# Attention and a mixture of experts on one core: the PSUM banks of sums and of turned sums in one pool of six

## The chip, the cores and the metric

The kernel runs on one core of a Trainium2 chip. The metric is the device time of one execution in microseconds (us); the median of three runs before the change is 2277.7 us (2277.5 to 2278.34). A measured change of less than about 0.2% can't be told from none.

## The reference

```python
def _attn_ref(u, v, z):                     # u, v: (8, 2496, 256), z: (8, 2496, 64)
    scores = (1.0 / S) * np.matmul(z, z.transpose(0, 2, 1))
    attn = np.maximum(scores, 0.0) ** 2
    return u * np.matmul(attn, v)

def _moe_ref(x, modality_id, w_gate, modality_bias, w1, w2):   # x: (19968, 256), 8 experts, F = 1024
    logits = x @ w_gate + modality_bias[modality_id]
    e_idx = np.argmax(logits, axis=1)
    probs = softmax(logits); gate_w = probs[np.arange(N), e_idx]
    for e in range(E):
        mask = e_idx == e
        h = np.maximum(x[mask] @ w1[e], 0.0)
        out[mask] = gate_w[mask, None] * (h @ w2[e])
```

The rows that the attention gives are the tokens of the experts.

## The kernel before

**The attention** runs over 8 batches of 2496 rows. A batch is cut into 5 chunks of queries, four of 512 columns and a last of 448, and every chunk goes through 10 steps over the keys, two key tiles of 128 a step (`i` from 0 to 9). A step has

- six score matmuls (`scores`, L280) into the two banks of the pool `ps_s`, issued three steps ahead of their use;
- on ScalarE the ReLU out of these banks (L288) and the square (L294);
- the split of the squares into a high and a low part, `ah` (L310, on ScalarE or VectorE) and `al` (L319, VectorE);
- 24 products (`weigh`, L335) with the high and low parts of `v`, summed over the 10 steps. They have 64 rows of contraction each, so two run at a time, one on either half of the array. There are four sums for a chunk, each in a bank of 512 float32: the two halves `r` of the contraction by the two halves `dh` of the 256 output rows.

At the first step of a chunk (`i == 0`) the products stand in the order of `dh`: twelve into the two sums of `dh = 0`, then twelve into those of `dh = 1`. That is the **change of chunk**. Around it stand, in this order on each engine:

- ScalarE, at the end of the old chunk: `evacuate_low` (L379) copies the two sums with `r = 1` to SBUF, `h = 0` first;
- VectorE, in the first step of the new chunk: `evacuate_high` (L383) adds the two sums with `r = 0` to these copies, `h = 1` first and `h = 0` last;
- TensorE, after the 24 products of that step: `make_rows` (L413) turns the sum by 16 transposes into two more banks, which VectorE reads in the next step (`take_rows`, L423).

Then come logits (L435), routing for each batch (`route_count` on TensorE, L512, into two banks, read by `route_slots`, L518 and L520) and the scatter of the rows to DRAM.

**The experts** follow: tiles of 512 tokens, with `up` (L1006) and `down` (L1019, L1020), in pools of their own, `ps_h` and `ps_o`, which take over the eight banks. Four tiles of one expert run before the general ones; the turned sums of the attention's last chunk (`make_last_rows`, L395) are made after the second `up` of the first of them.

**Banks.** The core has eight banks. In the attention two belong to `ps_s`, four to `ps_a` (the sums, tag `acc`) and two to `ps_t` (tag `po`: turned sums, route counts, the first warming matmuls, and a second set of scores at three places near the start). A pool hands out the bank that was given back first. The first instruction that writes a new tile waits until the last reader of the bank's tile before it is done; TensorE runs its instructions in program order, so all that is behind waits too. The order of instructions on all engines is written by the program (a planner in the code sets it when the program is built).

Of the kernel before, what the change touches and what calls it, by code (L numbers as in the profile page):

```python
# [9 lines left out]
F32 = mybir.dt.float32  # L10
# [5 lines left out]
P = 128  # L16
T = 512
PSUM = bass.MemoryType.PSUM
# [8 lines left out]
def tile_attention_moe(ctx: ExitStack, tc: tile.TileContext, u, v, zt, mid, wg, mb, w1, w2, out):  # L27
# [15 lines left out]
    E, _, F = w1.shape  # L43
    N = B * S
    KD, KF = D // P, F // P
# [34 lines left out]
    ph1, feed = ExitStack(), ExitStack()  # L80
# [3 lines left out]
    bulk = ph1.enter_context(tc.tile_pool(name="bulk", bufs=1))  # L84
    raw = feed.enter_context(tc.tile_pool(name="raw", bufs=1, side="right"))
    ps_s = ph1.enter_context(tc.tile_pool(name="ps_s", bufs=1, space=PSUM))
    ps_a = ph1.enter_context(tc.tile_pool(name="ps_a", bufs=4, space=PSUM))
    ps_t = ph1.enter_context(tc.tile_pool(name="ps_t", bufs=2, space=PSUM))
    bank = {"pool": ps_t, "tag": "po"}

    def bank_tile(shape, name):
        return bank["pool"].tile(shape, F32, tag=bank["tag"], name=name)
# [171 lines left out]
    acc = {}  # L264

    def scores(g, more=False):

        b, c, i = steps[g]
        w = width[c]
        if more:  # L270
            s = [bank_tile([P, T], "s") for _ in halves]
        else:
            both = ps_s.tile([P, 2, T], F32, tag="s", name="s")
            s = [both[:, t, :] for t in range(2)]
        mv = Z[b, c]
        for n, (kl, ql) in enumerate(((0, 1), (1, 0), (0, 0)) if g else ((0, 0), (0, 1), (1, 0))):
            for t in range(2):
                k = 2 * i + t
                lhs = Z[b, k // J][halves[t], kl, (k % J) * P:(k % J + 1) * P]
                nc.tensor.matmul(out=s[t][:, :w], lhsT=lhs, rhs=mv[halves[t], ql, :w], start=n == 0, stop=n == 2)  # L280
        r = bulk.tile([P, 2, T], F32, tag="a", bufs=3, name="r")
        if more or not g:
            for t in range(2):
                nc.scalar.activation(out=r[:, t, :w], in_=s[t][:, :w], func=AF.Relu, scale=INV)  # L284
                if not g:
                    nc.scalar.square(out=r[:, t, :], in_=r[:, t, :])
        else:
            nc.scalar.activation(out=r[:, :, :w], in_=both[:, :, :w], func=AF.Relu, scale=INV)  # L288
        st_s[g] = r
# [37 lines left out]
    def weigh(g, inside=()):  # L327
        b, c, i = steps[g]
        w = width[c]
        ah, al = st_h.pop(g)  # L330
        if i == 0:
            acc[b, c] = list(zip(*([ps_a.tile([P, T], F32, tag="acc", name="acc") for _ in range(2)] for _ in range(KD))))

        def product(r, dh, k, x, y, stop=False):
            nc.tensor.matmul(  # L335
                out=acc[b, c][r][dh][:, :w],
                lhsT=V[b, k // J][y][halves[r], k % J, dh * P:(dh + 1) * P],
                rhs=x[halves[r], k % 2, :w],
                start=k == 0 and x is ah and not y,
                stop=stop,  # L340
            )


        last = i == NI - 1
        terms = [(dh, x, y) for dh in range(KD) for x, y in ((ah, 0), (ah, 1), (al, 0))]
        if i or not g:
            terms.sort(key=lambda t: (t[1] is al, t[2]))
        tiles = (2 * i, 2 * i + 1)[:1 if last else 2]
        for ks in (tiles,) if g else ((k,) for k in tiles):
            for m, (dh, x, y) in enumerate(terms):  # L350
                if m == len(terms) - KD and 2 * i in ks:
                    for n in inside:
                        scores(n, True)
                for k in ks:
                    for r in range(2):
                        product(r, dh, k, x, y)
        if last:

            k = NCOL - 1
            product(1, 0, k, al, 0, True)  # L360
            product(0, 1, k, ah, 0, True)
            product(1, 1, k, al, 0)
            product(0, 0, k, ah, 0)
            product(1, 1, k, ah, 1, True)
            product(0, 0, k, ah, 1, True)
# [517 lines left out]
    with tc.manual_schedule(engines={ET.PE, ET.Activation, ET.DVE, ET.Pool}):  # L883
# [44 lines left out]
        for g in range(G):  # L928
            waiting += [(end, g, p) for end, p in due.pop(g, ())]
            b, c, i = steps[g]  # L930
# [28 lines left out]
            for n in new_s:  # L959
                clock["A"] += 1.05 * scale  # L960
                square(n)
            weigh(g, inside)
            for n in inside:
                after += 0.69
# [244 lines left out]
```

## Time and profile before

| | |
|---|---|
| median of three runs | 2277.7 us |
| the profiled execution | 2277.82 us |
| its span, first to last instruction | 2276.0 us |
| end of the attention's products | about 1375 us |
| TensorE matmuls busy | 2247.5 us, 99% |
| weight loads (PEld) busy | 2029.5 us, 89% |
| VectorE busy | 1807.1 us, 79% |
| ScalarE busy | 1574.1 us, 69% |
| GpSimd busy | 360.6 us, 16% |
| mean granted clock of TensorE | 0.997 |

PE are TensorE's matmuls, PEld its weight loads, which run ahead of the matmuls that use them; DVE is VectorE, ACT ScalarE, POOL GpSimd. In a row `acc<-ah,vh` the tile ahead of the arrow is written, those behind it are read. Times in a timeline are counted from the start of the span; what stands in brackets is the idle time of the engine just ahead of the row and what ended it. A matmul's length counts from its start to its modelled end, so that two that overlap are both busy.

### The profile page before, as it was taken

To read this page: it belongs to the slowest core of one execution; us is meant where nothing else is said; L and a number is where in the kernel's file an instruction comes from. 1 tells how busy PE (TensorE), PEld (TensorE's weight loads), DVE (VectorE), ACT (ScalarE), POOL (GpSimd) and SP (SyncE) were. 2 spreads that over 40 slices of the span, in tenths; PEclk is the share of its full clock that TensorE was granted. 3 is DMA by queue.
4 is the path that set the end of the run, shared out by engine and by line. 5 is a ranking of instruction groups with operands and counts; after the bars stand their busy time and mean duration, and the time that the engine had idled before them with its cause. 6 is when DMAs were issued, how large, how long until landed. Compare 5 with 4: busy or idle time off the path is not lost.

```text
span 2276.0 us, 44472 instructions
## 1 busy us (share of the span) xinstructions
PE 2247.5 (99%) x16874; PEld 2029.5 (89%) x16874; DVE 1807.1 (79%) x4552; ACT 1574.1 (69%) x1917; POOL 360.6 (16%) x349
## 2 busy tenths in 40 slices
PE   9999999999999999999999999999999999999996
PEld 7999999999999999999989998888888888888885
DVE  7889989989989989989989889766666666666663
ACT  7888888888888888888888873455455455555452
POOL 0000210210210210210110321411212121212111
PEclk9999999999999999999999999999999999999998
DMA  6222222222112112112111122644545454545440
GB/s 186 105 69 92 89 87 95 92 70 74 37 53 73 38 53 72 38 54 72 38 49 35 53 87 51 190 133 146 140 138 154 125 166 117 162 121 158 128 144 23
DMA packets 199602, 216.64 MB, mean 95 GB/s; under 512 B 118448, under 2 KB 166064, under 8 KB 194512
## 3 DMA queue, kind: packets, MB, share of 16 engines
q1 hardware_dynamic: 184288, 172.49, 26.2%
q0 software_dynamic: 15088, 41.21, 4.9%
q8 instruction: 134, 2.20, 0.4%
q14 instruction: 92, 0.75, 0.1%
HBM read 168.23 MB, written 62.19 MB: 101 GB/s over the span
## 4 chain that ended last, share of the span: by engine, by line
PE 61%; issue 25%; DMA 9%; POOL 3%; ACT 1%; DVE 1%; POOLq 0%; ACTq 0%; DVEq 0%
PE acc L335 46%; PE s L280 12%; DMA out_dram<-y,ids 9%; POOL out_dram L1038 3%; PE ph L1006 1%; PE po L413 1%; PE po L1019 1%; ACT r L288 0%; ACT r L294 0%; DVE spare L435 0%; PE po L1020 0%; POOLq L1038 0%; PE warm L887 0%; ACT x L379 0%; ACT r L284 0%
## 5 line engine op out<-in xcount | busy, mean ns | idle before, releaser
L288 ACT ACTIVATE r<-s 128x1024 f32<-128x1024 f32 (+1 forms) x395 | 397.9, 1007 | 217.1 <-PE s L280 216.8
L335 PE MATMUL acc<-ah,vh 64*128 64x512 f32 (+1 forms) x3120 | 530.1, 387 | 8.4 <-ACT x L379 7.1
L319 DVE TENSOR_TENSOR al<-r,ah 128x1024 fp32r<-128x1024 f32 (+1 forms) x359 | 430.3, 1199 | 111.5 <-ACT ah L310 96.9
L335 PE MATMUL acc<-ah,vl 64*128 64x512 f32 (+1 forms) x3120 | 511.8, 382 | 0.0
L335 PE MATMUL acc<-al,vh 64*128 64x512 f32 (+1 forms) x3120 | 506.7, 382 | 0.0
L435 DVE SCALAR_TENSOR_TENSOR spare<-x,wgb 128x256 f32<-128x256 f32 x1280 | 461.9, 419 | 1.0
L1010 ACT ACTIVATE hh<-ph 128x512 fp32r<-128x512 f32 x312 | 186.6, 598 | 386.7 <-PE ph L1006 346.2
L1019 PE MATMUL po<-w,hh 128*128 128x512 f32 x1256 | 450.0, 394 | 0.0
L335 PEld LDWEIGHTS acc<-ah,vh 64*128 64x128 f32 x3120 | 399.7, 184 | 48.0 <-ACT x L379 32.3
L1006 PE MATMUL ph<-xh,w 128*128 128x512 f32 x1248 | 429.9, 395 | 0.0
L294 ACT ACTIVATE r<-r 128x1024 f32<-128x1024 f32 (+1 forms) x399 | 415.8, 1042 | 3.5
L335 PEld LDWEIGHTS acc<-ah,vl 64*128 64x128 f32 x3120 | 403.6, 184 | 14.0
L335 PEld LDWEIGHTS acc<-al,vh 64*128 64x128 f32 x3120 | 403.0, 184 | 14.2
L280 PE MATMUL s<-zm 64*128 64x512 f32 (+1 forms) x2400 | 405.7, 385 | 0.8 <-ACT r L288 0.3
L1011 DVE SCALAR_TENSOR_TENSOR hl<-ph,hh 128x512 fp32r<-128x512 f32 x312 | 215.3, 690 | 218.1 <-ACT hh L1010 189.6
L548 POOL DMA_INDIRECT xs<-x,sloti x160 | 200.8, 1255 | 1052.5 <-DVE x L546 1006.9
L1020 PE MATMUL po<-w,hl 128*128 128x256 f32 x1256 | 351.5, 280 | 0.2 <-DVE hl L1011 0.2
L280 PEld LDWEIGHTS s<-zm 64*128 64x128 f32 x2400 | 310.8, 185 | 8.5 <-ACT r L288 0.8
L310 ACT CAST ah<-r 128x1024 fp32r<-128x1024 f32 (+1 forms) x283 | 288.1, 1018 | 0.0
L1019 PEld LDWEIGHTS po<-w,hh 128*128 128x128 f32 x1256 | 235.7, 188 | 55.4
L1006 PEld LDWEIGHTS ph<-xh,w 128*128 128x128 f32 x1248 | 234.2, 188 | 55.9 <-issue 0.3
L1038 POOL DMA_INDIRECT out_dram<-y,ids x157 | 152.8, 973 | 692.3 <-DVE y L1036 657.8
(155 smaller groups left out, 1982.5 us busy)
## 6 DMA issues: line engine op xcount, KB each, us to landing
w<-w1s SPq DMA_DIRECT2D x37, 1024.0 KB
w<-w2s SPq DMA_DIRECT2D x37, 1024.0 KB
xg<-xs SPq DMA_DIRECT2D x156, 128.0 KB
vr<-in_v_dram SPq DMA_DIRECT2D x32, 512.0 KB
ut<-in_u_dram SPq DMA_DIRECT2D x32, 512.0 KB
zr<-in_zt_dram SPq DMA_DIRECT2D x40, 256.0 KB
w1s<-in_moe_w_dram SPq DMA_DIRECT2D x16, 512.0 KB
w2s<-in_moe_w_dram SPq DMA_DIRECT2D x8, 1024.0 KB
```

The source lines that it names most:

```text
L280: nc.tensor.matmul(out=s[t][:, :w], lhsT=lhs, rhs=mv[halves[t], ql, :w], start=n == 0, stop=n == 2)
L288: nc.scalar.activation(out=r[:, :, :w], in_=both[:, :, :w], func=AF.Relu, scale=INV)
L294: nc.scalar.square(out=a[:, :, :w], in_=a[:, :, :w])
L310: copy(out=ah[:, :, :w], in_=st_a[g][:, :, :w])
L319: nc.vector.tensor_tensor(out=al[:, :, :w], in0=a[:, :, :w], in1=ah[:, :, :w].bitcast(F32), op=ALU.subtract)
L335: nc.tensor.matmul(out=acc[b, c][r][dh][:, :w], lhsT=V[b, k // J][y][halves[r], k % J, dh * P:(dh + 1) * P], rhs=x[halves[r], k % 2, :w], ...
L435: nc.vector.scalar_tensor_tensor(out=spare[:, k % 2, :], in0=x[:, j, 0:D], scalar=1.0, in1=wgb[:, e, :], op0=ALU.mult, op1=ALU.mult, accum ...
L1006: nc.tensor.matmul(out=ph, lhsT=lhs, rhs=rhs[:, k, :], start=n == 0, stop=n == 3 * KD - 1)
L1011: nc.vector.scalar_tensor_tensor(out=hl, in0=ph, scalar=0.0, in1=hh.bitcast(F32), op0=ALU.max, op1=ALU.subtract)
L1019: nc.tensor.matmul(out=po[j], lhsT=hh[:, s], rhs=both, start=f == 0, stop=False, skip_group_check=True)
L1020: nc.tensor.matmul(out=po[j][:, 0:D], lhsT=hl[:, s], rhs=w[:, 0, :], start=False, stop=f == KF - 1, skip_group_check=True)
L1038: nc.gpsimd.indirect_dma_start(out=out, out_offset=bass.IndirectOffsetOnAxis(ap=ids[:, j:j + 1], axis=0), in_=y, in_offset=None, bounds_ch ...
```

## The change

```diff
-    ps_a = ph1.enter_context(tc.tile_pool(name="ps_a", bufs=4, space=PSUM))
-    ps_t = ph1.enter_context(tc.tile_pool(name="ps_t", bufs=2, space=PSUM))
-    bank = {"pool": ps_t, "tag": "po"}
+    ps_a = ph1.enter_context(tc.tile_pool(name="ps_a", bufs=6, space=PSUM))
+    bank = {"pool": ps_a, "tag": "acc"}
...
         if i == 0:
-            acc[b, c] = list(zip(*([ps_a.tile([P, T], F32, tag="acc", name="acc") for _ in range(2)] for _ in range(KD))))
+            acc[b, c] = list(zip(*([bank_tile([P, T], "acc") for _ in range(2)] for _ in range(KD))))
```

The pools `ps_a` and `ps_t` become one of six banks, from which the sums, the turned sums, the route counts and the early scores all take the bank that was given back first. The program has one line less, so that L335 is L334 after the change, and so on. Every engine has the same instructions in the same order as before; what differs is the bank of a tile and with it what TensorE waits for. In the rows that follow, the engine that is waited for stands in brackets, and `x2` means two instructions alike.

TensorE at the change from the third to the fourth chunk of the first batch, before: six scores, 24 products, and the transposes into `po`.

```order
L280 MATMUL s<-zm 128x512 [waits Activation_49]
L280 MATMUL s<-zm 128x512 x5
L335 MATMUL acc<-ah,vh 128x512 [waits Activation_49] x2
L335 MATMUL acc<-ah,vh 128x512 x2
L335 MATMUL acc<-ah,vl 128x512 x4
L335 MATMUL acc<-al,vh 128x512 [waits DVE_49]
L335 MATMUL acc<-al,vh 128x512 x3
L335 MATMUL acc<-ah,vh 128x512 [waits DVE_49] x2
L335 MATMUL acc<-ah,vh 128x512 x2
L335 MATMUL acc<-ah,vl 128x512 x4
L335 MATMUL acc<-al,vh 128x512 x4
L413 MATMUL po<-ident,x 128x64 x16
```

The same place after the change:

```order
L279 MATMUL s<-zm 128x512 [waits Activation_49]
L279 MATMUL s<-zm 128x512 x5
L334 MATMUL acc<-ah,vh 128x512 x4
L334 MATMUL acc<-ah,vl 128x512 x4
L334 MATMUL acc<-al,vh 128x512 [waits DVE_49]
L334 MATMUL acc<-al,vh 128x512 x3
L334 MATMUL acc<-ah,vh 128x512 [waits Activation_49] x2
L334 MATMUL acc<-ah,vh 128x512 x2
L334 MATMUL acc<-ah,vl 128x512 x4
L334 MATMUL acc<-al,vh 128x512 x4
L412 MATMUL po<-ident,x 128x64 [waits DVE_49]
L412 MATMUL po<-ident,x 128x64 x15
```

The two waits for ScalarE's copies have moved from the first two products to the thirteenth and fourteenth, and the wait for VectorE's adds from these to the first transpose. It is so at all 39 changes of chunk; at six of them, each the first after a batch's route count, the first two products wait as well:

```order
L279 MATMUL s<-zm 128x512 x5
L334 MATMUL acc<-ah,vh 128x512 [waits DVE_49] x2
L334 MATMUL acc<-ah,vh 128x512 x2
L334 MATMUL acc<-ah,vl 128x512 x4
L334 MATMUL acc<-al,vh 128x512 [waits DVE_49]
```

What they wait for there is VectorE's reading of the counts (L518 and L520 of before). The last place is the end of the attention on TensorE: the last products, the first two `up` products of the first expert tile (six matmuls each) and the transposes of the last chunk; before the change

```order
L335 MATMUL acc<-ah,vl 128x448 x2
L1006 MATMUL ph<-xh,w_0_18698 128x512 [waits PE_49,Activation_49]
L1006 MATMUL ph<-xl,w_0_18698 128x512 [waits DVE_49]
L1006 MATMUL ph<-xh,w_0_18698 128x512 [waits DMAHW3_49]
L1006 MATMUL ph<-xh,w_0_18698 128x512 [waits Activation_49]
L1006 MATMUL ph<-xl,w_0_18698 128x512
L1006 MATMUL ph<-xh,w_0_18698 128x512 [waits DVE_49]
L1006 MATMUL ph<-xh,w_0_18698 128x512 [waits Activation_49]
L1006 MATMUL ph<-xl,w_0_18698 128x512
L1006 MATMUL ph<-xh,w_0_18698 128x512 x2
L1006 MATMUL ph<-xl,w_0_18698 128x512
L1006 MATMUL ph<-xh,w_0_18698 128x512
```

and after it:

```order
L334 MATMUL acc<-ah,vl 128x448 x2
L1005 MATMUL ph<-xh,w_0_18695 128x512 [waits PE_49,Activation_49]
L1005 MATMUL ph<-xl,w_0_18695 128x512 [waits DVE_49]
L1005 MATMUL ph<-xh,w_0_18695 128x512 [waits DMAHW3_49]
L1005 MATMUL ph<-xh,w_0_18695 128x512 [waits Activation_49]
L1005 MATMUL ph<-xl,w_0_18695 128x512
L1005 MATMUL ph<-xh,w_0_18695 128x512 [waits DVE_49] x2
L1005 MATMUL ph<-xl,w_0_18695 128x512
L1005 MATMUL ph<-xh,w_0_18695 128x512 x2
L1005 MATMUL ph<-xl,w_0_18695 128x512
L1005 MATMUL ph<-xh,w_0_18695 128x512
L394 MATMUL po<-ident,x 128x128 [waits Activation_49]
```

The seventh of these matmuls, the first of the second `up`, waited for ScalarE and now waits for VectorE: its bank held the sum with `r = 0`, `dh = 0` of the last chunk, which the last add (L383, `h = 0`) reads.

## The prediction

> **What bounds the kernel now.** First the page: span, busy shares and the 40 slices; then the waits, longest first; then the timeline at ordinary steps and at the change of chunk.
>
> ```profile
> span 2276.0 us, 44472 instructions
> ...
> PE 2247.5 (99%) x16874; PEld 2029.5 (89%) x16874; DVE 1807.1 (79%) x4552; ACT 1574.1 (69%) x1917; POOL 360.6 (16%) x349
> ...
> PEclk9999999999999999999999999999999999999998
> ```
>
> Then the windows view of the attention from its first change of chunk on (length, busy us of PE, PEld, DVE, ACT and POOL, granted clock, DMA share, GB/s):
>
> ```profile
> 42.00:1375.00 1333.00, 1325.75 (x12119) 1256.23 (x12117) 1181.27 (x3592) 1106.96 (x1222) 190.70 (x163) 1.00 0.21 67
> ```
>
> TensorE is busy 99% of the span, and in the attention 1325.75 of 1333 us with the full clock. That looks like nothing to gain. But a matmul that starts late while its predecessor drains still counts as busy, so busy time hides lost issue time. The waits show it (who <- for whom: total us, times, longest):
>
> ```profile
> ACT r L288 <- PE s L280: 216.8, 295, 2.5
> ...
> DVE al L319 <- ACT ah L310: 96.9, 120, 3.2
> ...
> PEld acc L335 <- ACT x L379: 32.3, 78, 1.4
> ...
> PE acc L335 <- ACT x L379: 7.1, 8, 0.9
> ...
> PEld acc L335 <- DVE x L383: 3.5, 16, 0.3
> ...
> PEld s L280 <- ACT r L288: 0.8, 1, 0.8
> ```
>
> ScalarE waits for TensorE (216.8 us), so TensorE sets the pace of the attention. TensorE itself waits at one place: the weight loads of the products (L335) wait 78 times, twice at each of the 39 changes of chunk, for ScalarE's copies of the previous chunk's sums (L379), and 16 times for VectorE's adds (L383). Together 32.3 + 3.5 = **35.8 us**. Whether those are lost is read from start to start. Two ordinary steps begin like this in the timeline, a step being six score matmuls and 24 products (start, length):
>
> ```profile
> 188.47 1.03 PE L280 MATMUL s<-zm 64*128 64x512 f32 x6
> ...
> 191.87 1.03 PE L280 MATMUL s<-zm 64*128 64x512 f32 x6
> ```
>
> So 30 matmuls of 512 columns take 3.40 us, 15 pairs of 0.227. Now a change of chunk:
>
> ```profile
> 284.72 1.03 PE L280 MATMUL s<-zm 64*128 64x512 f32 x6
> ...
> 285.10 1.05 ACT L379 COPY x<-acc 128x512 f32<-128x512 f32 x2
> ...
> 285.72 0.18 PEld L335 LDWEIGHTS acc<-ah,vh 64*128 64x128 f32 x1 [0.39 <-ACT x L379]
> ...
> 286.18 1.29 DVE L383 TENSOR_TENSOR x<-acc,x 128x512 f32<-128x512 f32 x2 [0.56 <-ACT x L379]
> 286.20 0.29 PEld L335 LDWEIGHTS acc<-ah,vh 64*128 64x128 f32 x3 [0.30 <-ACT x L379]
> ...
> 288.84 0.69 PE L413 MATMUL po<-ident,x 64*128 64x64 f32 x13
> ```
>
> From the scores to the transposes that follow the 24 products: 288.84 - 284.72 = 4.12 us instead of 3.40. The loss of 0.72 is the two waits, 0.39 + 0.30, and a little. Where ScalarE comes late, at the change of batch, more is lost:
>
> ```profile
> 178.91 1.22 DVE L250 TENSOR_TENSOR vl<-vr,vh 128x1024 fp32r<-128x1024 f32 x1
> ...
> 179.24 0.51 PE L335 MATMUL acc<-ah,vl 64*128 64x448 f32 x2
> 179.44 1.00 PE L280 MATMUL s<-zm 64*128 64x512 f32 x6
> ...
> 179.82 1.06 ACT L294 ACTIVATE r<-r 128x1024 f32<-128x1024 f32 x1
> ...
> 180.78 0.95 ACT L379 COPY x<-acc 128x448 f32<-128x448 f32 x2
> 181.35 0.18 PEld L335 LDWEIGHTS acc<-ah,vh 64*128 64x128 f32 x1 [1.34 <-ACT x L379]
> ...
> 181.77 1.16 DVE L383 TENSOR_TENSOR x<-acc,x 128x448 f32<-128x448 f32 x2 [0.50 <-ACT x L379]
> 181.79 0.29 PEld L335 LDWEIGHTS acc<-ah,vh 64*128 64x128 f32 x3 [0.25 <-ACT x L379]
> ...
> 184.47 0.69 PE L413 MATMUL po<-ident,x 64*128 64x64 f32 x13
> ...
> 186.11 1.03 ACT L288 ACTIVATE r<-s 128x1024 f32<-128x1024 f32 x1 [1.03 <-PE s L280]
> ```
>
> Here 184.47 - 179.44 = 5.03, a loss of 1.63 against waits of 1.34 + 0.25. So the idle of PEld at these waits is lost time nearly one to one, and the ceiling of the change is 35.8 us.
>
> **The change part by part.** No instruction is added, removed or moved; only the bank of each sum and what is waited for before its first matmul. At a change of chunk the first two new sums (rows dh=0) now take the two banks that held turned sums, the next two (dh=1) take the ones that ScalarE's copies free, and the turned sums take those that VectorE's adds free.
>
> *First two sums.* No wait is left: the turned sums are read (L423) in the step after they are written, most of a chunk ago. After a chunk with a route count the wait is for L518/L520, which read the counts:
>
> ```profile
> L520 DVE TENSOR_TENSOR base<-pc,base x17: 155/165/167, 243.9 to 1417.0; 128x8 f32<-128x8 f32 x17
> ...
> 250.93 0.18 PEld L335 LDWEIGHTS acc<-ah,vh 64*128 64x128 f32 x1 [0.39 <-ACT x L379]
> ```
>
> The first read of counts starts at 243.9, and the next chunk's first load stands at 250.93, or 0.7 earlier without its wait: about 6 us of cover. At a change of batch the second four products need a low part of `v`, written (L250) by 178.91 + 1.22 = 180.13 at the latest; without waits they come at 179.44 + 5 x 0.227 = 180.57. Cost nothing.
>
> *Last two sums.* They now wait for the copies, 12 products later. In the first example they are due at 284.72 + 9 pairs x 0.227 = 286.76, and the second copy released its bank by 286.20: 0.56 us of cover, so nothing is paid. At the change of batch they are due at 179.44 + 2.04 = 181.48, and the releases are at 181.35 and 181.79: the second one stays, some 0.3 us, less the 0.03 to 0.18 by which the second of a pair starts later anyway; I take 0.25. The seven changes of batch are of this kind, the first shown above and the last here, and one more change like them, at 1243.21:
>
> ```profile
> 1207.81 0.18 PEld L335 LDWEIGHTS acc<-ah,vh 64*128 64x128 f32 x1 [1.34 <-ACT x L379]
> ...
> 1243.21 0.18 PEld L335 LDWEIGHTS acc<-ah,vh 64*128 64x128 f32 x1 [1.19 <-ACT x L379]
> ```
>
> 8 x 0.25 = 2.0 us stay.
>
> *Turned sums.* The transposes now wait for VectorE's adds themselves, where before the products had waited. They read what the adds write, so no bank can be ready later than the data. In the first example the adds end at 286.18 + 1.29 = 287.47 and the transposes come to 284.72 + 3.40 = 288.12: cover 0.65. At the change of batch 182.93 against 183.09: cover 0.16, enough but thin. Behind this wait stand the next scores, so what is late here is paid in full; it would be what is late next.
>
> *What is late after that.* The next scores need the two banks of scores, read by L288; TensorE waited once for that in the whole run, 0.8 us. ScalarE's 216.8 us of waiting for scores shrink by what TensorE gains. VectorE is busy 1181.27 of 1333 us; with 33 us less it is at 91%, and no row of the waits has a product waiting for `al`, which is made three steps ahead.
>
> *End of the attention.* By the new banks the second up product of the first expert tile starts in the bank that the last add frees (it was one that a copy frees):
>
> ```profile
> 1375.65 0.50 PE L1006 MATMUL ph<-xh,w 128*128 128x512 f32 x1
> ...
> 1377.49 1.14 DVE L383 TENSOR_TENSOR x<-acc,x 128x448 f32<-128x448 f32 x2
> ...
> 1378.32 0.40 PE L1006 MATMUL ph<-xh,w 128*128 128x512 f32 x1
> 1378.69 0.86 PEld L395 LDWEIGHTS po<-ident,x 128*128 128x128 f32 x8 [0.41 <-DVE x L383]
> ```
>
> The first and the last of the twelve matmuls of two up products start 2.67 us apart, so one product of six takes about 1.4 us. The second ran while the adds did; now it must start after 1377.49 + 1.14 = 1378.63, and its 1.4 us stand ahead of the transposes of L395, which began at 1378.69. Lost once: 1.4 us, up to 2.0 if VectorE, with little slack there, does not follow the gain of the last chunk. I take 1.7.
>
> The sum: 35.8 - 2.0 - 1.7 = 32.1 us, all in the part before 1380 us. The expert part after it is TensorE back to back, its loads are issued at places of the same program, and it moves forward whole. The profiled execution took 2277.82 us (1.8 around its span), the median of the runs is 2277.7: 2277.8 - 32.1 = **2246** us, 1.4% less. Bounds: all 35.8 gives 2242; if the eight late changes keep their 1.6 us each for another reason (ScalarE's backlog), 12.8 - 2.0 = 10.8 more stays, 2257.
>
> A rule against the change: the Trainium skill, TensorE: Matmul & The Clock Gate, section HAM oscillation — how this bites in real kernels, tells of a kernel to which double buffering in PSUM gave no further gain (126.6 to 125.5 us). By it the sum would be nothing or up to 0.9%; there the wait was for a DMA, here the waits of TensorE name the evacuation, so I hold to the rows.
>
> **The rivals.**
> *Only what PE itself idled comes back.* The weight loads run ahead, so one could say that their 35.8 us lie beside running matmuls. Then the gain is the PE row of the waits, 7.1 us, less 1.7: 2272. Against it: the start-to-start losses of 0.72 and 1.63.
> *The late changes stay.* ScalarE is behind at the change of batch (L294 ends at 180.88, the chunk's last products at 179.75), and TensorE, let go 1.4 us earlier, meets that backlog at its next scores: the gain of these eight, 10.8 us, is paid there, and the time lies between 2251 (half of it) and 2257. For: the copies come 1.03 us after the products. Against: at 186.11, before the next scores but one, ScalarE has waited 1.03 us for scores again.
> *It does not do what it says.* A ring handed out in strict turn, six tiles a chunk (four and two), would give each sum the bank of its predecessor, with the old waits: 2278. Against it: in the order the waits have moved.
> *Slower.* Turning all sums over six banks makes the granted clock fall in the attention. Place: the steps after each change of chunk. Price: at a mean clock of 0.95 the 1333 us become 1403, and 2277.8 - 32 + 70 = 2316; it decides below 0.977, where 1333 us cost 32 more. Against it: the clock is 1.00 over the attention with gaps of up to 1.4 us, and the change shortens them. The Trainium skill, TensorE: Matmul & The Clock Gate, section A second HAM failure mode: psum-queue depth-cycling, tells of such a swing in a kernel that cycles through PSUM banks; no row of this trace has it.
>
> **How the numbers follow.** Forecast (2242 to 2251) 0.70; late changes stay (2251 to 2257) 0.13; only PE's idle 0.05; no effect 0.04; slower 0.04; 0.04 for a gain between the cases or over the ceiling, faster too. The range is 2241 to 2258, one us beyond the bounds since the durations are of one execution; it holds the first two, 0.83. About 0.2% (4.6 us) can be told from no change: faster 0.70 + 0.13 + 0.05 + 0.04 = 0.92, same 0.04, slower 0.04.
>
> **What would show it.** Right: the waits of L335's loads for L379 fall from 78 to about 8 and from 32.3 to about 2 us, those for L383 vanish; from scores to transposes 3.4 us at an ordinary change and about 3.65 at a change of batch; the attention ends some 32 us earlier, and a new wait of about 1.6 us for L383 stands before the second up product. Wrong: a wait for L288 or `al` in TensorE's rows, transposes waiting for L383, or a granted clock under 1.00 after a change of chunk.

## The result, and the profile after

| kernel | median us (lowest to highest, runs) | profiled execution's span | ratio to before (95% interval) |
|---|---|---|---|
| before | 2277.9 (2277.5 to 2278.3, 4) | 2276.0 | 1 |
| after | 2245.7 (2245.1 to 2245.8, 4) | 2243.9 | 0.9858 (0.9841 to 0.9875) |

The kernel is 32.2 us faster; 2246 was forecast. (The median of before now has a fourth run in it.) All lines of the kernel after stand one lower than before (L335 is L334, L379 is L378, L383 is L382, L413 is L412, L1006 is L1005). First the page of the kernel after:

```profile
span 2243.9 us, 44470 instructions
...
PE 2221.6 (99%) x16874; PEld 2020.7 (90%) x16874; DVE 1804.4 (80%) x4552; ACT 1573.0 (70%) x1917; POOL 366.3 (16%) x349
...
PEclk9999999999999999999999999999999999999998
```

TensorE's share is 99% as before, and the granted clock reads the same in every slice. The windows view of the attention from 42 us to its last products (length, busy us of PE, PEld, DVE, ACT and POOL, clock, DMA share, GB/s) says more:

```profile
42.00:1342.40 1300.40, 1300.06 (x12126) 1247.81 (x12123) 1179.09 (x3596) 1106.53 (x1223) 196.42 (x163) 1.00 0.21 68
```

The attention is 32.6 us shorter (1333.00 to 1300.40), though PE was busy for all but 7.25 us of it before and is now for all but 0.34. Of the 32.6 us only 6.9 had shown as idle PE; the other 25.7 had been hidden in "busy". The work of VectorE and ScalarE in it is the same to 2.2 and 0.4 us.

The waits of the kernel after (who <- for whom: total us, times, longest):

```profile
ACT r L287 <- PE s L279: 182.7, 274, 1.5
...
PEld acc L334 <- ACT x L378: 1.7, 7, 0.3
...
PE ph L1005 <- DVE x L382: 1.4, 1, 1.4
...
PEld po L412 <- DVE x L382: 0.8, 1, 0.8
```

The products' 78 waits for the copies are 7, and 32.3 us are 1.7; the products' 16 waits for the adds are gone. ScalarE waits 34.1 us less for scores (216.8 to 182.7), about what TensorE gained. Two waits are new, one each: the second up product at the end of the attention (L1005), and the turned sums at one change of chunk (L412). Beside them one weight load waits 0.18 us for a low part of `v` (L249), at 1207.20. The timeline shows three kinds of change: an ordinary one, one of batch, and the one at 1211.87.

```profile
279.31 1.01 PE L279 MATMUL s<-zm 64*128 64x512 f32 x6
279.66 1.05 ACT L378 COPY x<-acc 128x512 f32<-128x512 f32 x2
280.75 1.29 DVE L382 TENSOR_TENSOR x<-acc,x 128x512 f32<-128x512 f32 x2 [0.56 <-ACT x L378]
282.71 0.65 PE L412 MATMUL po<-ident,x 64*128 64x64 f32 x13
...
343.73 1.03 PE L279 MATMUL s<-zm 64*128 64x512 f32 x6
344.13 1.06 ACT L293 ACTIVATE r<-r 128x1024 f32<-128x1024 f32 x1
345.08 0.95 ACT L378 COPY x<-acc 128x448 f32<-128x448 f32 x2
346.09 0.29 PEld L334 LDWEIGHTS acc<-ah,vh 64*128 64x128 f32 x3 [0.25 <-ACT x L378]
347.38 0.63 PE L412 MATMUL po<-ident,x 64*128 64x64 f32 x11
...
1211.87 0.84 PE L279 MATMUL s<-zm 64*128 64x512 f32 x6
1212.85 1.06 ACT L378 COPY x<-acc 128x512 f32<-128x512 f32 x2
1213.48 1.22 DVE L318 TENSOR_TENSOR al<-r,ah 128x1024 fp32r<-128x1024 f32 x1
1214.62 1.28 DVE L382 TENSOR_TENSOR x<-acc,x 128x512 f32<-128x512 f32 x2
1215.96 0.53 PE L412 MATMUL po<-ident,x 64*128 64x64 f32 x10 [0.34 <-DVE x L382]
...
1344.54 1.14 DVE L382 TENSOR_TENSOR x<-acc,x 128x448 f32<-128x448 f32 x2
1345.74 0.50 PE L1005 MATMUL ph<-xh,w 128*128 128x512 f32 x1 [1.38 <-DVE x L382]
```

From the scores to the transposes the three take 3.40, 3.65 and 4.09 us; an ordinary change took 4.12 before (3.66 with 448 columns, now 3.04), one of batch 5.03. Six of the seven changes of batch now take 3.59 to 3.67, the one at 177.22 takes 3.45. At the first kind, now as short as an ordinary step, nobody waits. At the second the wait for the second copy is left, 0.25 us (0.17 at 177.22). At the third the copies are in time, but VectorE turns to its adds only at 1214.62, behind `al`, and the transposes stand for them. The last two rows are the end of the attention: the second up product waits 1.38 us for the adds.

### The profile page after: what moved, and what is told of

It reads as the page before. It is cut to its first block, busy times and chain, and to the rows that moved or that the text cites. A ratio compares the mean times of both kernels' runs of the same rounds, so it can differ in the third digit from the quotient of the medians.

```text
span 2243.9 us, 44470 instructions
## 1 busy us (share of the span) xinstructions
PE 2221.6 (99%) x16874; PEld 2020.7 (90%) x16874; DVE 1804.4 (80%) x4552; ACT 1573.0 (70%) x1917; POOL 366.3 (16%) x349
## 4 chain that ended last, share of the span: by engine, by line
PE 59%; issue 25%; DMA 9%; POOL 3%; DVE 3%; ACT 1%; POOLq 0%; DVEq 0%; ACTq 0%
PE acc L334 44%; PE s L279 12%; DMA out_dram<-y,ids 9%; POOL out_dram L1037 3%; DVE spare L434 1%; PE ph L1005 1%; PE po L412 1%; PE po L1018 1%; DVE al L318 1%; PE po L1019 0%; DVE vl L249 0%; POOLq L1037 0%; PE warm L886 0%; DVE ah L309 0%; DVE x L382 0%
## 5 line engine op out<-in xcount | busy, mean ns | idle before, releaser
L287 ACT ACTIVATE r<-s 128x1024 f32<-128x1024 f32 (+1 forms) x395 | 397.8, 1007 | 184.5 <-PE s L279 182.7
L334 PE MATMUL acc<-ah,vh 64*128 64x512 f32 (+1 forms) x3120 | 492.8, 383 | 1.0 <-DVE ah L301 1.0
L334 PE MATMUL acc<-ah,vl 64*128 64x512 f32 (+1 forms) x3120 | 487.0, 382 | 0.0
L334 PE MATMUL acc<-al,vh 64*128 64x512 f32 (+1 forms) x3120 | 483.8, 381 | 0.0
L1005 PE MATMUL ph<-xh,w 128*128 128x512 f32 x1248 | 430.1, 395 | 1.4 <-DVE x L382 1.4
L334 PEld LDWEIGHTS acc<-ah,vh 64*128 64x128 f32 x3120 | 383.3, 184 | 17.7 <-ACT x L378 1.7
L334 PEld LDWEIGHTS acc<-al,vh 64*128 64x128 f32 x3120 | 383.0, 184 | 14.6
L334 PEld LDWEIGHTS acc<-ah,vl 64*128 64x128 f32 x3120 | 381.3, 184 | 15.0 <-DVE vl L249 0.2
L279 PE MATMUL s<-zm 64*128 64x512 f32 (+1 forms) x2400 | 388.8, 386 | 0.8 <-ACT r L287 0.3
L547 POOL DMA_INDIRECT xs<-x,sloti x160 | 206.5, 1291 | 1016.2 <-DVE x L545 971.9
L279 PEld LDWEIGHTS s<-zm 64*128 64x128 f32 x2400 | 292.6, 185 | 12.3 <-ACT r L287 0.8
L1005 PEld LDWEIGHTS ph<-xh,w 128*128 128x128 f32 x1248 | 234.2, 188 | 57.6 <-DVE x L382 1.8
```

The lines of the kernel that those rows point to most:

```text
L334: nc.tensor.matmul(out=acc[b, c][r][dh][:, :w], lhsT=V[b, k // J][y][halves[r], k % J, dh * P:(dh + 1) * P], rhs=x[halves[r], k % 2, :w], ...
L1005: nc.tensor.matmul(out=ph, lhsT=lhs, rhs=rhs[:, k, :], start=n == 0, stop=n == 3 * KD - 1)
```

## The experiments

Ten kernels, in three groups; each group ran beside the kernel before (medians 2278.27, 2277.97 and 2277.82). Costs below are differences of medians, against the kernel before of the same group, or against the kernel after's 2245.7, which was measured in none of these groups. Differences from the kernel after under 4.6 us (0.2%) can't be told from none by the medians: for e2, e5, e6, e8 and e9 it is the rows of the traces that carry the reading. The theory: TensorE waited in the open for the evacuation of the sums at each change of chunk, and the ring puts 12 products between the scores and the first sum that needs a bank which is still being read. The rivals: only PE's own idle came back; the late changes are ScalarE's backlog; the saving has nothing to do with when the copies end.

| run | edit | forecast us | measured us (lowest to highest) | ratio to before (95%) |
|---|---|---|---|---|
| e1 | before, copies late | 2290 | 2293.7 (2292.3 to 2293.9) | 1.0066 (1.0049 to 1.0082) |
| e2 | after, copies late | 2248 | 2248.5 (2247.9 to 2248.9) | 0.9868 (0.9852 to 0.9885) |
| e3 | after, copies later | 2264 | 2273.7 (2272.2 to 2274.6) | 0.9980 (0.9970 to 0.9989) |
| e4 | half a ring | 2251 | 2254.6 (2253.6 to 2255.1) | 0.9895 (0.9878 to 0.9911) |
| e5 | after, last adds first | 2244.5 | 2244.6 (2243.9 to 2245.1) | 0.9854 (0.9839 to 0.9869) |
| e6 | after, copies first at batch | 2243.9 | 2242.7 (2240.9 to 2243.4) | 0.9845 (0.9831 to 0.9858) |
| e7 | before, copies first at batch | 2272.0 | 2271.6 (2270.4 to 2272.6) | 0.9973 (0.9962 to 0.9985) |
| e8 | after, e5 and e6 | 2242.7 | 2241.9 (2241.6 to 2242.9) | 0.9843 (0.9829 to 0.9856) |
| e9 | after, adds late | 2247.8 to 2250 | 2249.8 (2248.2 to 2251.0) | 0.9875 (0.9858 to 0.9891) |
| e10 | before, adds late | 2289 to 2299 | 2297.1 (2296.4 to 2298.0) | 1.0085 (1.0068 to 1.0102) |

### The same delay of the copies in both kernels: e1, e2

```diff
+        if not h:
+            nc.scalar.copy(out=oT[b, c][0][:, h, :256], in_=acc[b, c][1][h][:, :256])
         nc.scalar.copy(out=oT[b, c][0][:, h, :w], in_=acc[b, c][1][h][:, :w])
```

> The kernel before, with one more ScalarE copy of 256 columns ahead of the two copies of the finished sums at each of the 40 chunks (the same values are written twice), so that both copies end later by d, some 0.3 us by the rows of the 512-column copies. Theory (TensorE waits in the open for the copies at each change of chunk): the delay is paid in full at 39 changes, 39 x 0.3 = 12 us, so 2290 us, and the waits of the products' loads for the copies grow from 32.3 to about 44 us. Rival (the copies are not what holds TensorE, the gain came from elsewhere): ScalarE has 217 us of idle time, the delay is swallowed, 2278 us.

> The kernel after, with the same added copy. Theory (the wait for the copies now has some 0.56 us of cover at an ordinary change and none at the eight late ones): 31 ordinary changes hide the 0.3 us, eight pay it, 8 x 0.3 = 2.4 us, so 2248 us; the ratio of this run's cost to that of the same edit in the kernel before is about 1 to 5. Rival (no cover, the ring saved a fixed time at each change): the edit costs here what it costs in the kernel before, some 12 us, 2258 us.

An ordinary change of e1 in the timeline, and its waits (two fences, the first the timeline):

```profile
287.81 1.02 PE L280 MATMUL s<-zm 64*128 64x512 f32 x6
288.18 0.35 ACT L380 COPY x<-acc 128x256 f32<-128x256 f32 x1
288.57 1.07 ACT L381 COPY x<-acc 128x512 f32<-128x512 f32 x2
289.20 0.18 PEld L335 LDWEIGHTS acc<-ah,vh 64*128 64x128 f32 x1 [0.79 <-ACT x L381]
289.69 0.29 PEld L335 LDWEIGHTS acc<-ah,vh 64*128 64x128 f32 x3 [0.30 <-ACT x L381]
...
292.34 0.34 PE L415 MATMUL po<-ident,x 64*128 64x64 f32 x3
```

```profile
PEld acc L335 <- ACT x L381: 48.2, 78, 1.7
```

The added copy puts off the others by 288.57 - 288.18 = 0.39 us. The change takes 292.34 - 287.81 = 4.53 us instead of 4.12, the first wait has grown from 0.39 to 0.79, and the whole run is 15.4 us slower: 39 x 0.39 = 15.2. Summed from scores to transposes, the 39 changes take 15.1 us more. Before, then, this lateness of the copies is paid in full, with 217 us of idle time on ScalarE and a PE that is 99% busy. In the kernel after the same copy costs 2.8 us. Its ordinary change, and its waits:

```profile
279.46 1.02 PE L279 MATMUL s<-zm 64*128 64x512 f32 x6
...
282.87 0.53 PE L414 MATMUL po<-ident,x 64*128 64x64 f32 x9
```

```profile
PEld acc L334 <- ACT x L380: 4.9, 16, 0.4
```

282.87 - 279.46 = 3.41: an ordinary change pays nothing. The waits are 3.2 us more than the kernel after's 1.7, 2.6 of them at the seven changes of batch, which take 3.9 to 4.1 us instead of 3.4 to 3.7, and 0.5 at the late change that waits for VectorE anyway, where they cost nothing (4.08 us). About one to six for the same edit: the rival without cover (2258) is out.

### How much cover: e3

```diff
+        if not h:
+            for _ in range(2):
+                nc.scalar.copy(out=oT[b, c][0][:, h, :w], in_=acc[b, c][1][h][:, :w])
         nc.scalar.copy(out=oT[b, c][0][:, h, :w], in_=acc[b, c][1][h][:, :w])
```

> The kernel after, with two more full copies ahead of the two (three times the first one), a delay of about 0.95 us, beyond the cover of 0.56. Theory: an ordinary change pays 0.95 - 0.56 = 0.4 us less up to 0.1 by which the second of a pair starts later anyway, 31 x 0.35 = 11 us, and the eight late ones pay it whole, 8 x 0.95 = 7.6 us: 2264 us, and waits for the copies of some 20 us. With a cover twice as long as I read it the 31 would pay nothing: 2253. Without any cover: 39 x 0.95 = 37 us, 2283.

The 28 us lie between the theory's 18 and the 37 of no cover, so the timeline has to say which number was off:

```profile
284.14 0.95 PE L279 MATMUL s<-zm 64*128 64x512 f32 x6
284.43 1.19 ACT L380 COPY x<-acc 128x512 f32<-128x512 f32 x2
285.65 1.07 ACT L381 COPY x<-acc 128x512 f32<-128x512 f32 x2
286.29 0.18 PEld L334 LDWEIGHTS acc<-ah,vh 64*128 64x128 f32 x1 [0.27 <-ACT x L381]
286.77 0.29 PEld L334 LDWEIGHTS acc<-ah,vh 64*128 64x128 f32 x3 [0.30 <-ACT x L381]
288.10 0.71 PE L415 MATMUL po<-ident,x 64*128 64x64 f32 x14
```

The copies end at 285.65 + 1.07 - 284.14 = 2.58 us after the scores, and did so at 279.66 + 1.05 - 279.31 = 1.40: the delay is 1.18, not the 0.95 that I took. The change takes 3.96 instead of 3.40 and pays 0.56. The cover is 1.18 - 0.56 = 0.62 us, next to the 0.56 of the forecast. It was the edit that I mis-sized, not the cover. The waits of the products for the copies are 27.9 us, 26.2 more than in the kernel after, and that is the most part of the 28.

### A part of the ring: e4

Only the dh=0 sums and the turned sums share banks (four); the dh=1 sums keep two of their own.

```diff
-    ps_a = ... tile_pool(name="ps_a", bufs=4, ...)
-    ps_t = ... tile_pool(name="ps_t", bufs=2, ...)
+    ps_a = ... tile_pool(name="ps_a", bufs=2, ...)
+    ps_t = ... tile_pool(name="ps_t", bufs=4, ...)
...
-            acc[b, c] = list(zip(*([ps_a.tile(...) for _ in range(2)] for _ in range(KD))))
+            low = [bank_tile([P, T], "acc") for _ in range(2)]
+            acc[b, c] = list(zip(low, [ps_a.tile(...) for _ in range(2)]))
```

> A part of the change: only the sums of dh=0 and the turned sums share a ring (of four banks); the two sums of dh=1 keep two banks of their own, which VectorE's first add and ScalarE's second copy free. Theory (two thirds and more of the loss was the first two sums' wait; a sum of dh=1 has 12 products ahead of it): the dh=1 sum that waits for the first add is due at 2.04 us and the add ends at 1.9 to 2.1 at an ordinary change, 0 to 0.1 us each, but at 2.95 at the seven changes of batch, 0.65 more than with the full ring, and 0.7 at the change at 1211: 4.6 + 0.7 + 1 - 0.6 (the second up product's bank is freed by the first add) = 5.7 more than the ring of six, 2251 us. Rival (all four sums have to be in the ring, each wait is worth the same): half the gain, 2262.

The waits of e4:

```profile
PEld acc L336 <- DVE x L384: 10.1, 35, 0.7
...
PEld acc L336 <- ACT x L380: 3.1, 8, 0.4
```

It keeps 23.7 of the 32 us, so the first two sums' freedom from waits gives about three quarters of the gain, and the rival with half is out by 7 us. The dh=1 sum that needs the bank of VectorE's first add waits at 35 changes. From scores to transposes a change of batch takes 4.3 us, about 0.67 more than in the full ring (0.65 forecast), and a 512-column change 0.1 more on average: 2.3 us over 23 of them and 0.4 over the eight of 448 columns, where I had said 1 for all. The late change at 1219.95 takes 0.34 more, where I had said 0.7. That is some 1.3 of the 3.6 us beyond the forecast's 2251; the rest is not traced. Where the other two banks come from is thus worth something at nearly every change.

### The same delay of the adds in both kernels: e9, e10

```diff
         y = oT[b, c][0][:, h, :width[c]]
+        if h:
+            nc.vector.tensor_copy(out=y, in_=y)
         nc.vector.tensor_tensor(out=y, in0=acc[b, c][0][h][:, :width[c]], in1=y, op=ALU.add)
```

> The kernel after, with a copy of 512 columns in place (the same values written again) ahead of VectorE's two adds at each of the 40 chunks, which then end later by d, between 0.35 us (half of the 1024-column cast's 0.69) and 0.65 us (the 512-column copy of L180). Theory (the transposes wait for the adds with a cover of 0.65 us at an ordinary change and 0.15 at a change of batch): the 31 others hide it, seven changes of batch pay d - 0.15, the change at 1211 and the end of the attention pay d: with d = 0.35 that is 2.1 us, 2247.8; with d = 0.6 it is 4.4 us, 2250. Rival (the transposes are bound to the adds at every change, no cover): 40 x d, 14 to 26 us, 2260 to 2272.

> The kernel before, with the same added copy ahead of the adds. Theory (one of the dh=1 sums waits for the bank that the second add frees, due 2.75 us after the scores, and the add ends 2.75 us after them): each change pays d less some 0.05, 39 x 0.3 = 12 us with d = 0.35, 2290; with d = 0.6 21 us, 2299. Rival (only the copies hold TensorE before, the adds are beside the path): 2278.

A change of batch in the timeline of e9, then the waits of e9 and, in a fence of their own, those of e10:

```profile
344.11 0.86 PE L279 MATMUL s<-zm 64*128 64x512 f32 x6
346.29 0.40 DVE L383 COPY x<-x 128x448 f32<-128x448 f32 x1 [0.58 <-ACT x L378]
346.79 1.16 DVE L384 TENSOR_TENSOR x<-acc,x 128x448 f32<-128x448 f32 x2
348.00 0.71 PE L414 MATMUL po<-ident,x 64*128 64x64 f32 x16
```

```profile
PEld po L414 <- DVE x L384: 4.9, 10, 1.3
```

```profile
PEld acc L335 <- ACT x L379: 31.6, 76, 1.3
PEld acc L335 <- DVE x L385: 17.4, 49, 0.4
```

The delay is 346.79 - 346.29 = 0.50 us (0.53 with 512 columns). In e9 the transposes wait at ten places, the change of batch takes 348.00 - 344.11 = 3.89 (0.24 more), and the ordinary changes 3.40 as ever. Of VectorE's half us the ring hides all at 31 changes and about half at seven; the change that is now at 1213.87 pays it whole. That makes 2.5 us at the changes, and the up product behind the attention waits 1.89 us instead of 1.38: 3.0 in all. The median is 4.1 us slower, and the other 1.1 goes with the clock: two executions with a mean granted clock of 0.997 took 2248.2 and 2248.7 us, two with 0.996 took 2250.9 and 2251.0. The profiled one is of the second kind; its clock is 0.50 from 1350.29 to 1353.70 us, soon after the up product's wait, and 1.00 on both sides. Why it fell there is open.

In the kernel before the same copy costs 19.3 us, 18.3 of them at the changes: 0.43 to 0.59 us at 32 of them and 0.28 to 0.38 at the seven of batch, which have a little room. Elsewhere the fourth sum's bank came from the second add just as it was needed, and the waits for the adds go from 3.5 to 17.4 us. VectorE's adds were nearly as much on the path before as ScalarE's copies, and the prediction's 3.5 us for them was only what stood out behind the copies.

### What was left: e5, e6, e7, e8

e5 issues VectorE's last two adds ahead of the last step's logits:

```diff
+            if g == G - 1:
+                for h in reversed(range(KD)):
+                    evacuate_high(b, c, h)
             beside(g, False)
             now = after
         assert not tasks
-        for h in reversed(range(KD)):
-            evacuate_high(B - 1, NCH - 1, h)
```

e6 (on the kernel after) and e7 (on the kernel before) put ScalarE's square behind its copies at the changes of batch; e8 is e5 and e6 together:

```diff
             for n in new_s:
                 clock["A"] += 1.05 * scale
-                square(n)
+                if i < NI - 1 or c < NCH - 1:
+                    square(n)
...
+            if i == NI - 1 and c == NCH - 1:
+                for n in new_s:
+                    square(n)
             beside(g, False)
             now = after
```

> The kernel after, with the last two adds of the attention issued ahead of the logits of the last step on VectorE instead of behind them (five logits of 0.42 stood between the copies and the adds). Theory (the second up product of the first expert tile now starts in the bank that the last add frees, and lost 1.4 us there): the adds follow the copies at once, end at about 1344.5 instead of 1345.7, the up product waits 0.2 us or less, and the transposes of the expert part begin 1.2 us earlier: 2244.5 us. Rival (the expert part is held by something else there, such as its loads or the logits): 2245.7.

> The kernel after, with ScalarE's copies of the finished sums issued ahead of a square of 1.06 us (not behind it) at the seven changes of batch. Theory (the 0.2 to 0.27 us that stay there are the second copy's lateness, ScalarE working off that square first): the copies end 0.85 us earlier, the seven changes take 3.4 instead of 3.65 us from scores to transposes, 7 x 0.25 = 1.75 less: 2243.9 us, and the waits of the products for the copies vanish. Rival (the change of batch is late for another reason, the low parts of v or the next scores): 2245.7.

> The kernel before, with the same exchange at the seven changes of batch. Theory (ScalarE's copies hold TensorE there in the open): the loss of 1.63 at each falls by the 0.85 to 0.95 us that the copies come earlier, to an ordinary change's 0.72: 7 x 0.9 = 6.3 less, 2272.0 us. Rival (ScalarE's backlog itself holds the change, so that the copies' order is nothing): 2278.2.

> The kernel after with both exchanges, of VectorE's last adds and of ScalarE's copies at the changes of batch. Theory: the two gains stand at different places and add up, 1.2 + 1.75 = 2.95 less than the kernel after, 2242.7 us. Rival (one of them is an ordinary cost that turns up later): 2244 or more.

The end of the attention in e5, a change of batch in e6, and the waits of e7, a fence each:

```profile
1342.05 0.97 ACT L378 COPY x<-acc 128x448 f32<-128x448 f32 x2 [3.81 <-PE acc L334]
...
1343.05 1.16 DVE L382 TENSOR_TENSOR x<-acc,x 128x448 f32<-128x448 f32 x2 [0.17 <-ACT x L378]
...
1344.26 0.51 PE L1006 MATMUL ph<-xh,w 128*128 128x512 f32 x1 [0.25 <-DVE x L382]
```

```profile
342.98 0.86 PE L279 MATMUL s<-zm 64*128 64x512 f32 x6
343.21 0.97 ACT L378 COPY x<-acc 128x448 f32<-128x448 f32 x2
...
346.41 0.66 PE L412 MATMUL po<-ident,x 64*128 64x64 f32 x16
```

```profile
PEld acc L335 <- ACT x L379: 25.5, 77, 1.2
PEld acc L335 <- DVE x L383: 5.3, 23, 0.3
PE acc L335 <- ACT x L379: 0.8, 1, 0.8
```

*e7* settles the seven changes of batch: with nothing but the order of a square and two copies, the kernel before gains 6.4 us (6.3 forecast), and PE's idle for the copies falls from 7.1 to 0.8. What ScalarE's backlog cost there was the lateness of the two copies. *e5*: the adds end at 1344.21 instead of 1345.68, the up product waits 0.25 instead of 1.38 us, the transposes of the experts begin 1.48 us earlier, 0.35 of it from the attention, which ended that much earlier in this execution, and the median is 1.1 us lower (1.2 forecast). *e6*: the copies come 0.23 us after the scores (1.35 before the exchange), the change takes 346.41 - 342.98 = 3.43 us instead of 3.65, and no wait for the copies is left. Of its 3.0 us, 1.3 are at these changes (0.16 to 0.24 at six, 0.02 at the first, which had little to lose) and 0.35 at the change at 1208.98, where the adds come earlier too; 0.7 already stood before the first change of batch, where the two programs do not differ, and is the start of that execution; the rest is spread over the attention and not traced. *e8*, with 2241.9, is the fastest of all and 36.1 us under the kernel before. Its interval overlaps that of the kernel after; the ranges of their runs (2241.6 to 2242.9, 2245.1 to 2245.8) do not. e8 and e6 are not told apart by time, though the up product's wait is as short in e8 as in e5.

## Why the prediction was right, and where its terms were off

*The ceiling.* That the idle of PEld at the change of chunk is lost one to one (35.8 us) was the step that carried the forecast. It is borne out by e1 and e10: a delay of 0.39 us in the copies cost 15.1 us over the 39 changes, one of 0.50 to 0.53 in the adds 18.3, with some room left at the seven changes of batch. The size was 1.0 too high: from start to start the 39 changes of before lost 34.8 us beyond 3.40 each (3.04 with 448 columns), so that not every wait was lost whole. At a 448-column change, for one, waits of 0.17 + 0.30 + 0.21 cost 0.63. The rival by which only PE's own idle comes back (2272) fell with the result: the attention lost 32.6 us of length and only 6.9 us of idle PE.

*First two sums, last two sums.* No wait for the first two, and a cover of 0.56 us for the last two: e2 pays nothing at ordinary changes with a delay of 0.39, and e3 gives 0.62. The residual of 0.25 at a change of batch was 0.19 to 0.27 at six of the seven; at the first it was 0.05.

*The eighth late change* is the mis-sized term. The one at 1243.21 (1211.87 now) was counted like a change of batch, with 0.25 us left for ScalarE's second copy. There the copies are in time, and VectorE is what is late, with `al` and a row of logits ahead of its adds: 4.09 - 3.40 = 0.69 us. It is the wait of the transposes that the prediction named as the next to be late, and among its signs of being wrong; it came at one change of 39, at another place than the change of batch, where its cover of 0.16 held (e9: half of a 0.50 delay hidden). The prediction worked that cover out for the two other kinds of change and not for this one, where the trace of before already had it missing:

```profile
1241.44 1.01 PE L280 MATMUL s<-zm 64*128 64x512 f32 x6
...
1243.85 1.28 DVE L383 TENSOR_TENSOR x<-acc,x 128x512 f32<-128x512 f32 x2
```

The adds end at 1243.85 + 1.28 = 1245.13, and without waits the transposes come at 1241.44 + 3.40 = 1244.84.

*End of the attention.* The new wait is there, at the named place. It was put at 1.7 us and is 1.38; the transposes of the experts begin 1378.69 - 1347.24 = 31.45 us earlier and the last products 1375.18 - 1342.39 = 32.8.

*The sum.* Forecast 35.8 - 2.0 - 1.7 = 32.1. From start to start the traces show 34.8 - 2.2 - 1.4 = 31.2, about the 31.45 us by which the transposes come earlier; the last 0.7 of the 32.2 lie behind them and are not traced. The terms were off by 1.0, 0.2 and 0.3 us. That the mechanism and the size of the gain came out was no luck; that the sum meets the measurement to a tenth of a us was.

*Late changes stay* (2251 to 2257): fell with the kernel after, and e7 shows the mechanism at the seven changes of batch. *Does not do what it says*: the waits moved as the banks did. *Slower by the clock*: the granted clock is 0.997 over the run in the kernel after, as before, and in the attention 1.00, as in the profile of every run here. The Trainium skill, TensorE: Matmul & The Clock Gate, section A second HAM failure mode: psum-queue depth-cycling, describes clock swings in a kernel that cycles through PSUM banks; here sums and turned sums go round six banks 40 times, and no profile shows one in the attention. The one drop that a profile shows ahead of its last 16 us is that of e9, 3.4 us long, behind the attention.

*The rule against the change*, from the same page of the Trainium skill, section HAM oscillation — how this bites in real kernels (double buffering in PSUM gave that kernel no further gain): here more banks in turn gave 1.4%. This agrees with the Trainium skill, Perfetto Trace Analysis, section Matmuls: matmul groups should rotate through PSUM banks so that the evacuation of one lies beside the matmuls of the next. What told the cases apart beforehand was whom the waits of TensorE named: a DMA there, by the page's account of that kernel's loop, the evacuation of a bank here.

## What to carry to other kernels

A busy engine can still be losing time at its waits: look at the starts of the same instruction in two steps, and if the difference equals the idle of the weight loads, count that idle and not the gaps of the matmuls. When tiles of different lives share a pool, the first one needed should get the bank that has been free longest; how much lateness that hides is worked out from due time less release, and is measured by putting the same delay into both kernels. What is left is then at the few places where an engine's order puts something else ahead of an evacuation. At two kinds of them an exchange of instructions took out most of it here (e5, e6); the late change at 1211.87 kept 0.34 us.

## What had not been expected

The prices of two extra copies, back to back on ScalarE: a 256-column copy put off the next by 0.39 us, and two of 512 columns by 1.18, more than the 1.06 that a pair takes from start to end (e1, e3).

The start of the kernel differs from execution to execution: the scores of the first change of chunk stand at 43.62 us in the kernel after and at 42.96 in e6, whose program is the same up to there. With differences of 1 to 3 us, as in e5 to e8, such 0.7 us have to be taken out place by place.
